# Weight halves by q and k, ten layer-norm applies on GpSimd, and a last tile in two PSUM banks: one change to a one-core attention-plus-gMLP kernel

## The chip, the cores and the metric

The kernel runs on one core of one Trainium2 chip. The metric is the device time of one execution in microseconds (us). The profile and the trace are of one profiled execution; they cover the span from the first to the last instruction, which is mostly about 1.7 us shorter than the device time. Five engines matter: TensorE (PE, with its weight loads PEld), VectorE (DVE), ScalarE (ACT), GpSimd (POOL) and SyncE (SP), which issues most DMAs (transfers; one "lands" when its data is in place). PSUM is the memory into which TensorE writes its results.

Here a run counts as slow when it is more than 1.5% above the fastest run of the same kernel.

## The reference, cut to what matters

```python
x = A_x                                   # [1, 2048, 512] bf16
xn = _layernorm(x, axis=-1, eps=1e-05)
return x + _A_ref(xn, A_wqkv, A_wo) + _B_ref(xn, B_w_in, B_w_sp, B_b_sp, B_w_out)
# _A_ref: qkv = xn @ wqkv; 32 heads of 16; each position attends to 8 positions, 2 apart; softmax; @ wo
# _B_ref: z = gelu(xn @ w_in); z2 = layernorm(second half); (z1 * (w_sp @ z2 + b)) @ w_out
```

## The kernel before

The 16 tiles of 128 tokens are taken in four blocks of four tiles (block j holds tiles j, j+4, j+8, j+12). A tile passes through batch-norm statistics, square root, reciprocal and the *apply* (subtract the mean, multiply by the reciprocal), then a transpose to `xnT`. Six tiles are transposed by TensorE and copied out of PSUM by ScalarE, the other ten by DMA transposes from SP. TensorE then multiplies `xnT` with the q/k weights (tile `pq`), later with the z2 weights (`pz`). VectorE multiplies q with shifted k (the *products*, into `r_pr`), and TensorE sums those into logits (`pl`).

```python
def load_wqk(E, h):                       # half h: q and k columns of chunks 2h, 2h+1
    ...
    for s in range(2):
        E.dma_start(w[:, :, s, 2 * h:2 * h + 2, :], src[:, :, s, 2 * h:2 * h + 2, :])

load_wqk(SP, 0)
SP.dma_start(xall[:, 1], xblk[1])
load_wqk(SP, 1)
for j in range(2, 4):
    SP.dma_start(xall[:, j], xblk[j])
SP.dma_start(w_z2[:], ...)
# ... [cut]
def ln_apply(i):
    j, tb = i % 4, i // 4
    V.tensor_scalar(xall[:, j, tb, :], xall[:, j, tb, :], mv[:, i, 0:1], rstd[:, i:i + 1],
                    ALU.subtract, ALU.mult)
def tr_dma(i):
    SP.dma_start_transpose(xnT[:, :, i * P:(i + 1) * P], xall[:, j, tb, :])
# ... [cut: first block]
qk_part(pqs[1], 0, 1, 0, 2)
tr_copy(t0[3], tr(t0[3]))
qk_part(pqs[2], 0, 2, 0, 2)               # stands between the 4th tile's transposes and their readers
# ... [cut]
ln_stats_blk(2)
ln_recip(blk_cols(2))
for i in blk(2):
    ln_apply(i)
    tr_dma(i)
# ... [cut: q/k of block 1, block 3 in the same way]
for c in range(C):                        # the products start
    prod_c(0, c)
    prod_c(1, c)
z2s(0, 0)
z2s(0, 1)
for c in range(C):
    qk_mm(2, c)                           # needs all four tiles of block 2
logits(0)
logits(1)
# ...
qk_mm(3, 0)                               # needs all four tiles of block 3
# ... [cut: the last tile's output]
store(3, A, slice(0, D // 2))             # two adds after the last matmul
store(3, SP, slice(D // 2, D))
```

Of the kernel before, what the change touches and what calls it, by code (L numbers as in the profile page):

```python
# [8 lines left out]
F32 = mybir.dt.float32  # L9
I32 = mybir.dt.int32  # L10
ACT = mybir.ActivationFunctionType
ALU = mybir.AluOpType
# [3 lines left out]
P = 128  # L16
S = 2048
D = 512
NT = S // P
TB = 4  # L20
TBS = 512
C = D // P
# [4 lines left out]
HALO = 16  # L27
F = 1376
FH = 688
FHALF = 344  # L30
MCH = 7
FPAD = MCH * P
FULL = (MCH - 2) * P
KR = (FH - FULL) // 2
# [7 lines left out]
APPLY_PER_G = [1, 2, 3, 4, 4, 4, 4, 4, 4, 6, 6, 6, 4, 4, 3, 1]  # L42
OUT_AFTER = [8, 12, 15.5]
NZ1 = 8


def slot_w(s):
# [4 lines left out]
def kernel(  # L52
# [13 lines left out]
    V = nc.vector  # L66
    A = nc.scalar
    G = nc.gpsimd
    PE = nc.tensor
    SP = nc.sync  # L70
# [7 lines left out]
    ps_mm = ctx.enter_context(tc.tile_pool(name="ps_mm", bufs=3, space=PSUM))  # L78
# [5 lines left out]
    xall = r_x[:, 0:4 * TB * D].rearrange("p (j b d) -> p j b d", j=4, b=TB)  # L84
    vp = r_x[:].rearrange("p (d t) -> p d t", d=DH)
    r_w = sb.tile([P, 8192], BF16, name="r_w")
    wqk = r_w[:, 0:4096].rearrange("p (k f) -> p k f", k=C)
    wv = r_w[:, 4096:6144].rearrange("p (k h d) -> p k d h", k=C, d=DH)
    a_sb = r_w[:, 0:4096].rearrange("p (w t) -> p w t", w=W)
    wout = r_w[:, 4096:4096 + MCH * D].rearrange("p (m n) -> p m n", m=MCH)  # L90
    r_qk = sb.tile([P, 2 * C * (HALO + S)], BF16, name="r_qk")
    qk = r_qk[:].rearrange("p (c s t) -> p c s t", s=2, c=C)
    wsp = [r_qk[:, n * 2048:(n + 1) * 2048].rearrange("p (k t) -> p k t", k=NT) for n in range(NWSP)]
    xr_t = [r_qk[:, NWSP * 2048 + n * D:NWSP * 2048 + (n + 1) * D] for n in range(4)]
    ot_t = [r_qk[:, NWSP * 2048 + (4 + n) * D:NWSP * 2048 + (5 + n) * D] for n in range(4)]
    r_lg = sb.tile([P, W * TBS], F32, name="r_lg")
    lg = r_lg[:].rearrange("p (w o t) -> p w o t", w=W, o=4)
    wo_r = r_lg[:].bitcast(BF16).rearrange("p (d n) -> p d n", d=DH)
# [3 lines left out]
    op = r_pr[:, 8192:16384].rearrange("p (d t) -> p d t", d=DH)  # L102

    xnT = sb.tile([P, C, S], BF16, name="xnT")
    w_z2 = sb.tile([P, C, FH], BF16, name="w_z2")
    w_z1 = sb.tile([P, C, FH], BF16, name="w_z1")
    z2 = sb.tile([P, NT, FH], BF16, name="z2")
    z1u = sb.tile([P, NZ1, FPAD], BF16, name="z1u")
    smt = sb.tile([P, 4, 256], F32, name="smt")
    uT = sb.tile([P, 2, MCH, TBS], BF16, name="uT")  # L110
# [8 lines left out]
    mv = sb.tile([P, NT, 2], F32, name="mv")  # L119
    rstd = sb.tile([P, NT], F32, name="rstd")  # L120
# [9 lines left out]
    def load_x0(E, tb, p0=0, p1=P):  # L130
        E.dma_start(xall[p0:p1, 0, tb, :], x2[tb * TBS + p0:tb * TBS + p1, :])  # L131

    def load_wqk(E, h):

        w = wqk.rearrange("p k (s c f) -> p k s c f", s=2, c=C)
        src = A_wqkv[:, 0:2 * D].rearrange("(k p) (s c f) -> p k s c f", p=P, s=2, c=C)
        for s in range(2):
            E.dma_start(w[:, :, s, 2 * h:2 * h + 2, :], src[:, :, s, 2 * h:2 * h + 2, :])  # L138

    load_x0(SP, 0, 0, 64)  # L140
    load_x0(A, 0, 64, P)
# [6 lines left out]
    load_wqk(SP, 1)  # L148
    for j in range(2, 4):
        SP.dma_start(xall[:, j], xblk[j])  # L150
    SP.dma_start(w_z2[:], B_w_in[:, FH:F].rearrange("(k p) f -> p k f", p=P))


    V.memset(warm[:], 0.0)
# [26 lines left out]
    def ln_recip(sl):  # L181
        V.reciprocal(rstd[:, sl], rstd[:, sl])

    def ln_apply(i):
        j, tb = i % 4, i // 4
        V.tensor_scalar(xall[:, j, tb, :], xall[:, j, tb, :], mv[:, i, 0:1], rstd[:, i:i + 1],
                        ALU.subtract, ALU.mult)

    def tr(i):
        j, tb = i % 4, i // 4  # L190
        pt = ps_aux.tile([P, C, P], BF16, name="pt", tag="aux")
        for c in range(C):
            PE.transpose(pt[:, c, :], xall[:, j, tb, c * P:(c + 1) * P], ident[:])  # L193
        return pt

    def tr_copy(i, pt):
        A.copy(xnT[:, :, i * P:(i + 1) * P], pt[:])  # L197
# [54 lines left out]
    def z1_mm(n):  # L252
        i = 4 * (n % 4) + ORD[n // 4]
        pz = zmm(i, w_z1)
        z = 32 * (n % 4)
        A.activation(z1u[:, n % NZ1, z:z + FH].rearrange("p (a b) -> p a b", a=2), pz[:, :, 0:FHALF],  # L256
                     ACT.Gelu_apprx_tanh)

    def qk_part(pq, j, c, b0, b1):

        xv = xnT[:].rearrange("p k (b j t) -> p k b j t", b=TB, j=4)
        for s in range(2):
            for kc in range(C):
                PE.matmul(pq[:, s, b0 * P:b1 * P], wqk[:, kc, s * D + c * P:s * D + (c + 1) * P],  # L264
                          xv[:, kc, b0:b1, j, :], start=(kc == 0), stop=(kc == C - 1))

    def qk_copy(pq, j, c):
        dst = qk[:, c, :, HALO:HALO + S].rearrange("p s (b j t) -> p s b j t", b=TB, j=4)
        A.copy(dst[:, :, :, j, :], pq[:].rearrange("p s (b t) -> p s b t", b=TB))  # L269

    def qk_tile():
        return ps_mm.tile([P, 2, TBS], F32, name="pq", tag="mm")

    def qk_mm(j, c):
        pq = qk_tile()
        qk_part(pq, j, c, 0, TB)
        qk_copy(pq, j, c)
# [105 lines left out]
    def u_mul(n, gs):  # L383
        s = n % NZ1
        g = gs[:].rearrange("p a b -> p (a b)")

        z = 32 * (n % 4)
        V.tensor_tensor(z1u[:, s, 0:FULL], g[:, 0:FULL], z1u[:, s, z:z + FULL], ALU.mult)
        rest = z1u[:, s, FULL:FPAD].rearrange("p (a q) -> p a q", a=2)[:, :, z:z + KR]
        V.tensor_tensor(rest, g[:, FULL:FH].rearrange("p (a q) -> p a q", a=2),  # L390
                        z1u[:, s, z + FULL:z + FH].rearrange("p (a q) -> p a q", a=2), ALU.mult)
        SP.dma_start_transpose(uT[:, (n // 4) % 2, :, (n % 4) * P:(n % 4 + 1) * P], z1u[:, s, :])
# [6 lines left out]
    def out_mm(o, last=False):  # L399
        pos = []  # L400
        for tb in range(TB):
            if last and tb >= 2:
                pa = ps_aux.tile([P, TBS], F32, name="pa", tag="aux")
                pos.append(pa[:])
                continue
            if tb % 2 == 0:
                pmm = ps_mm.tile([P, 2, TBS], F32, name="po", tag="mm")
            pos.append(pmm[:, tb % 2, :])
        for d in range(DH):
            for tb in range(TB):  # L410
                PE.matmul(pos[tb], op[32 * tb:32 * tb + 32, d, o * P:(o + 1) * P],  # L411
                          wo_r[32 * tb:32 * tb + 32, d, :],
                          start=(d == 0), stop=False, tile_position=(32 * tb, 0))
        for rt in range(2):
            for tb in range(TB):
                q, m = 32 * tb, MCH - 2 + rt
                PE.matmul(pos[tb], uT[q:q + KR, o % 2, m, tb * P:(tb + 1) * P], wout[q:q + KR, m, :],  # L417
                          start=False, stop=False, tile_position=(q, 0))

        def store(tb, E, cs):  # L420
            i = 4 * tb + ORD[o]
            V.tensor_tensor(ot_t[tb][:, cs], pos[tb][:, cs], xr_t[tb][:, cs], ALU.add)  # L422
            E.dma_start(out2[i * P:(i + 1) * P, cs], ot_t[tb][:, cs])

        for h in range(2):
            pair = (2 * h, 2 * h + 1)
            alone = last and h == 1
            for tb in pair:
                for m in range(MCH - 2):
                    PE.matmul(pos[tb], uT[:, o % 2, m, tb * P:(tb + 1) * P], wout[:, m, :],  # L430
                              start=False, stop=(m == MCH - 3))
                if alone and tb == 2:
                    store(2, SP, slice(0, D))
            if alone:
                store(3, A, slice(0, D // 2))
                store(3, SP, slice(D // 2, D))
            else:
                for tb in pair:
                    store(tb, SP, slice(0, D))


    pwm = ps_aux.tile([P, TBS], F32, name="pwm", tag="aux")
# [1 line left out]
    def blk(j):  # L444
        return [4 * tb + j for tb in range(TB)]

    def col(i):
        return slice(i, i + 1)
# [18 lines left out]
    def warm_up(n):  # L467
        for _ in range(n):
            PE.matmul(pwm[:], warm[:, 0:P], warm[:], start=True, stop=True)

    def ln_tile(i):
        ln_recip(col(i))
        ln_apply(i)

    t0, i1 = blk(0), blk(1)
    warm_up(9)
    for n in range(2):
# [2 lines left out]
    for n in range(2):  # L480
        ln_tile(t0[n])
        tr_copy(t0[n], tr(t0[n]))
        if n == 0:
            warm_up(2)
    for n in range(2, 4):
        ln_stats(t0[n])
        ln_sqrt(col(t0[n]))
    for n in range(2, 4):
        ln_tile(t0[n])
    pqs = [qk_tile() for _ in range(3)]  # L490
    qk_part(pqs[0], 0, 0, 0, 2)
    tr_copy(t0[2], tr(t0[2]))
    qk_part(pqs[1], 0, 1, 0, 2)
    tr_copy(t0[3], tr(t0[3]))
    qk_part(pqs[2], 0, 2, 0, 2)
    for n in range(2):
        ln_stats(i1[n])
    ln_sqrt(slice(1, 8, 4))
# [1 line left out]
    ln_recip(slice(1, 8, 4))  # L500
    ln_apply(i1[0])
    ln_apply(i1[1])
    ln_stats(i1[3])
    qk_part(pqs[0], 0, 0, 2, 4)
    qk_copy(pqs[0], 0, 0)
    ln_sqrt(slice(9, 16, 4))
    ln_recip(slice(9, 16, 4))
    for n in range(2, 4):
        ln_apply(i1[n])
        tr_dma(i1[n])  # L510
    qk_part(pqs[1], 0, 1, 2, 4)
    qk_copy(pqs[1], 0, 1)
    for n in range(2):
        tr_copy(i1[n], tr(i1[n]))
    qk_part(pqs[2], 0, 2, 2, 4)
    qk_copy(pqs[2], 0, 2)
    qk_mm(0, 3)
    ln_stats_blk(2)
    ln_recip(blk_cols(2))
    for i in blk(2):  # L520
        ln_apply(i)
        tr_dma(i)
    pqs = [qk_tile() for _ in range(3)]
    for c in range(3):
# [6 lines left out]
            ln_recip(blk_cols(3))  # L531
    qk_mm(1, 3)
    for i in blk(3):
        ln_apply(i)
        tr_dma(i)
    SP.dma_start(r_w[:, 4096:6144].rearrange("p (k f) -> p k f", k=C),
                 A_wqkv[:, 2 * D:3 * D].rearrange("(k p) f -> p k f", p=P))
# [80 lines left out]
    for n in range(NT):  # L618
        o = n // 4
# [43 lines left out]
```

## Time and profile before

| | before |
|---|---|
| device time, median of the first 3 runs | 210.86 us (210.77 to 211.06) |
| profiled span | 209.3 us |
| PE busy | 202.7 us, 97% |
| DVE busy | 176.9 us, 85% |
| POOL busy | 5.7 us, 3% |

The page of the kernel before: the span, the engines' busy times, and the busy tenths in 40 slices of 5.2 us. PEclk is the granted TensorE clock in tenths.

```profile
span 209.3 us, 4186 instructions
...
PE 202.7 (97%) x1727; PEld 121.3 (58%) x1731; DVE 176.9 (85%) x267; ACT 92.9 (44%) x148; POOL 5.7 (3%) x21
...
PE   7799999999999999999999999999999999999993
...
POOL 7000001100000000000000000000000000000000
PEclk9999999999999999999999999999999999999999
```

TensorE is full from the third slice to the last but one, at full clock. The chain of waits of the kernel before says the same in order of time (start, length, what):

```profile
4.61 6.68 DMA r_w<-in_A_wqkv_dram
...
11.34 2.36 PE pq L264 x20
...
14.14 9.57 PE pq L264 x72
23.71 2.41 PE pz L207 x16
```

From 11.34 us on, every step of the chain is TensorE work, down to 206 us, but for gaps of at most 0.16 us.

The timeline of the kernel before (start, length, engine, line, operation, tiles, shapes, count; in brackets the idle time before and what ended it). These are lines, each from the list of its engine:

```profile
13.98 9.73 PE L264 MATMUL pq<-xnT,r_w 128*128 128x256 bf16 x72
23.54 2.57 PE L207 MATMUL pz<-w_z,xnT 128*128 128x344 bf16 x16
...
34.96 1.90 PE L264 MATMUL pq<-xnT,r_w 128*128 128x512 bf16 x8
...
24.09 1.38 DVE L186 TENSOR_SCALAR r_x<-r_x,mv,rstd 128x512 bf16<-128x512 bf16 x4
25.39 3.49 DVE L287 TENSOR_TENSOR r_pr<-r_qk 128x2048 bf16<-128x2048 bf16 x3
...
14.84 14.88 SPq L201 DMA_TRANSPOSE xnT<-r_x  x10
```

The last block's four applies take VectorE 1.38 us together (0.41 us for one by itself), then the products start (the list is cut at 28 us; the first products run on after it). All ten DMA transposes are issued by 29.7 us; the last q/k matmuls that need them start at 34.96.

The tail on VectorE before, the last line of its list (two adds):

```profile
206.01 0.76 DVE L422 TENSOR_TENSOR r_qk<-pa,r_qk 128x256 bf16<-128x256 f32 x2 [0.27 <-PE pa L430]
```

### The profile page before, as it was taken

How to read it: one execution, taken by the hardware profiler on the slowest of the kernel's cores; microseconds unless marked ns; L12 is line 12 of the kernel's file. 1: busy time of each engine (PE TensorE's matmuls, PEld its weight loads, DVE VectorE, ACT ScalarE, POOL GpSimd, SP SyncE). 2: the span in 40 equal slices, each digit the busy share in tenths (PEclk: the TensorE clock that was granted, in tenths of full speed). 3: DMA queues.
4: the chain of work that ended last, by engine and by line, in shares of the span. 5: the costliest groups of instructions: out<-in, count | busy, mean ns of one | idle time of the engine just before them, and what ended most of it. 6: DMA issues, size and time to landing. Idle time of an engine off the chain costs nothing.

```text
span 209.3 us, 4186 instructions
## 1 busy us (share of the span) xinstructions
PE 202.7 (97%) x1727; PEld 121.3 (58%) x1731; DVE 176.9 (85%) x267; ACT 92.9 (44%) x148; POOL 5.7 (3%) x21
## 2 busy tenths in 40 slices
PE   7799999999999999999999999999999999999993
PEld 2578644545566566666666666456666446664441
DVE  3888997969999987999999999859999979991404
ACT  3475797788997897941431223102123102231000
POOL 7000001100000000000000000000000000000000
PEclk9999999999999999999999999999999999999999
DMA  4984556000000499799999776994833234424153
GB/s 132 326 281 66 101 94 232 0 0 3 0 3 0 103 179 210 146 280 216 177 191 218 129 161 145 147 194 150 126 76 89 47 94 150 47 45 89 51 152 100
DMA packets 66914, 25.91 MB, mean 124 GB/s; under 512 B 56080, under 2 KB 66768, under 8 KB 66768
## 3 DMA queue, kind: packets, MB, share of 16 engines
q1 hardware_dynamic: 66304, 25.20, 56.1%
q10 hardware_dynamic: 592, 0.46, 0.7%
q8 instruction: 13, 0.21, 0.4%
q14 instruction: 5, 0.04, 0.1%
HBM read 10.13 MB, written 2.10 MB: 58 GB/s over the span
## 4 chain that ended last, share of the span: by engine, by line
PE 93%; DMA 3%; SPq 2%; issue 1%; DVE 0%; DVEq 0%
PE pg L377 36%; PE pz L207 18%; PE pq L264 12%; PE po L430 7%; PE po L411 7%; PE pv L342 7%; PE pl L304 4%; DMA r_w<-in_A_wqkv_dram 3%; PE pa L430 1%; PE po L417 1%; SPq L138 1%; SPq L131 1%; SPq L147 0%; PE pt L193 0%; DVE r_qk L422 0%
## 5 line engine op out<-in xcount | busy, mean ns | idle before, releaser
L377 PE MATMUL pg<-z,r_qk 128*128 128x344 bf16 x512 | 76.8, 309 | 0.0
L377 PEld LDWEIGHTS <-r_qk 128*128 128x128 bf16 x512 | 50.0, 98 | 24.9 <-issue 0.4
L207 PE MATMUL pz<-w_z,xnT 128*128 128x344 bf16 x256 | 40.9, 309 | 0.0
L380 ACT ACTIVATE gs<-pg,b_col 128x688 bf16<-128x688 f32 x16 | 13.3, 832 | 57.0 <-PE pg L377 50.1
L353 DVE TENSOR_TENSOR r_pr<-r_x,r_w 128x2048 bf16<-128x2048 bf16 x32 | 38.1, 1221 | 0.3
L357 DVE TENSOR_TENSOR r_pr<-r_pr 128x2048 bf16<-128x2048 bf16 x28 | 33.8, 1219 | 0.1
L207 PEld LDWEIGHTS <-xnT 128*128 128x128 bf16 x256 | 24.6, 98 | 14.7 <-issue 2.0
L264 PE MATMUL pq<-xnT,r_w 128*128 128x256 bf16 (+1 forms) x176 | 29.4, 321 | 0.8 <-ACT xnT L197 0.7
L297 DVE TENSOR_TENSOR r_pr<-r_qk 128x2048 bf16<-128x2048 bf16 x24 | 27.5, 1218 | 2.8 <-ACT r_qk L269 2.8
L264 PEld LDWEIGHTS <-r_w 128*128 128x128 bf16 x176 | 16.8, 98 | 11.5 <-issue 1.8
L422 DVE TENSOR_TENSOR r_qk<-po,r_qk 128x512 bf16<-128x512 f32 x14 | 9.0, 686 | 15.6 <-PE po L430 15.6
L256 ACT ACTIVATE z1u<-pz 128x688 bf16<-128x688 f32 x16 | 11.9, 742 | 20.8 <-PE pz L207 20.7
L269 ACT CAST r_qk<-pq 128x1024 bf16<-128x1024 f32 x16 | 15.8, 1012 | 5.8 <-PE pq L264 4.3
L430 PE MATMUL po<-r_w,uT 128*128 128x512 bf16 x66 | 14.9, 379 | 0.6 <-issue 0.6
L342 PE MATMUL pv<-xnT,r_w 128*32 128x512 bf16 x256 | 14.7, 380 | 0.0
L411 PE MATMUL po<-r_lg,r_pr 32*128 32x512 bf16 x224 | 14.5, 375 | 0.0
L430 PEld LDWEIGHTS <-uT 128*128 128x128 bf16 x80 | 7.5, 98 | 10.2 <-issue 1.7
L175 DVE BATCH_NORM_STATS2 stats<-r_x 128x6 f32<-128x512 bf16 x16 | 10.8, 672 | 2.3 <-DMA r_x<-in_A_x_dram 2.1
L219 ACT ACTIVATE junk<-z 128x688 bf16<-128x688 bf16 x16 | 12.4, 778 | 0.5
L213 ACT ACTIVATE z<-pz 128x688 bf16<-128x688 f32 x16 | 11.8, 736 | 1.9 <-PE pz L207 1.9
L342 PEld LDWEIGHTS <-r_w 128*32 128x32 bf16 x256 | 9.5, 139 | 4.5 <-issue 0.3
L411 PEld LDWEIGHTS <-r_pr 32*128 32x128 bf16 x256 | 6.2, 93 | 7.7 <-issue 1.3
(67 smaller groups left out, 136.3 us busy)
## 6 DMA issues: line engine op xcount, KB each, us to landing
r_lg<-in_A_wo_dram SPq DMA_DIRECT2D x4, 512.0 KB, 9.0
r_qk<-in_A_x_dram SPq DMA_DIRECT2D x16, 128.0 KB, 2.2
out_dram<-r_qk SPq DMA_DIRECT2D x15, 128.0 KB, 1.7
r_x<-in_A_x_dram SPq DMA_DIRECT2D x3, 512.0 KB, 6.0
w_z<-in_B_w_in_dram SPq DMA_DIRECT2D x2, 688.0 KB, 5.3
r_w<-in_A_wqkv_dram SPq DMA_DIRECT2D x4, 256.0 KB, 6.4
r_w<-in_B_w_out_dram SPq DMA_DIRECT2D x1, 640.0 KB, 5.6
r_w<-in_A_wqkv_dram SPq DMA_DIRECT2D x1, 512.0 KB, 4.0
```

Of the source, the lines that this page charges most:

```text
L207: PE.matmul(pz[:, hh, 0:FHALF], xnT[:, kc, i * P:(i + 1) * P], wz[:, kc, hh * FHALF:(hh + 1) * FHALF], start=(kc == 0), stop=(kc == C - 1))
L219: A.activation(junk[:], z2[:, i, :], ACT.Square, accum_out=zsq[:, q:q + 1])
L264: PE.matmul(pq[:, s, b0 * P:b1 * P], wqk[:, kc, s * D + c * P:s * D + (c + 1) * P], xv[:, kc, b0:b1, j, :], start=(kc == 0), stop=(kc == C ...
L269: A.copy(dst[:, :, :, j, :], pq[:].rearrange("p s (b t) -> p s b t", b=TB))
L297: V.tensor_tensor(pr[g % 2][:, :, ww], q4, k4, ALU.mult)
L342: PE.matmul(pv[32 * tb:32 * tb + 32, dd, :], wv[:, kc, 2 * d2 + dd, :], xnT[:, kc, tb * TBS:(tb + 1) * TBS], start=(kc == 0), stop=(kc == ...
L353: V.tensor_tensor(pw_t[n], vp[:, :, off:off + P], a_sb[:, slot_w(w), ts].unsqueeze(1).broadcast_to([P, DH, P]), ALU.mult)
L357: V.tensor_tensor(pw_t[n] if dst is None else dst, pw_t[n], pw_t[m], ALU.add)
L377: PE.matmul(pg[:, hh, 0:FHALF], wsp[n % NWSP][:, k, :], z2[:, k, hh * FHALF:(hh + 1) * FHALF], start=(q == 0), stop=(q == NT - 1))
L380: A.activation(gs[:], pg[:, :, 0:FHALF], ACT.Identity, bias=b_col[:, i:i + 1])
L411: PE.matmul(pos[tb], op[32 * tb:32 * tb + 32, d, o * P:(o + 1) * P], wo_r[32 * tb:32 * tb + 32, d, :], start=(d == 0), stop=False, tile_po ...
L430: PE.matmul(pos[tb], uT[:, o % 2, m, tb * P:(tb + 1) * P], wout[:, m, :], start=False, stop=(m == MCH - 3))
```

## The change

Its intent: load the q/k weights as two column halves, q and then k (rows of 1 KB instead of 512 B, two loads fewer), and let TensorE begin with q alone; take ten applies off VectorE, which is 85% busy, and give them to GpSimd, which is idle; issue the z2 weights after the second block's transposes; and split the last tile's output over two PSUM banks, so that most of its add runs before the last matmul. Cut to its core:

```diff
-    def load_wqk(E, h):
-        ...
-        for s in range(2):
-            E.dma_start(w[:, :, s, 2 * h:2 * h + 2, :], src[:, :, s, 2 * h:2 * h + 2, :])
+    def load_wqk(E, s):
+        E.dma_start(wqk[:, :, s * D:(s + 1) * D], A_wqkv[:, s * D:(s + 1) * D]...)
     ...
-    SP.dma_start(w_z2[:], ...)                      # moved, see below
     ...
-    def ln_apply(i):
+    def ln_apply(i, E=V):
-        V.tensor_scalar(...)
+        E.tensor_scalar(...)
     ...
+    LN_E = G
     ...
-        if n == 0:
-            warm_up(2)
     ...
+    halves = [(0, 0), (0, 2), (1, 0)]               # q chunks 0,1; q 2,3; k 0,1
-    qk_part(pqs[0], 0, 0, 0, 2)
+    qk2_part(pqs[0], *halves[0], 0, 2)
+    qk2_part(pqs[1], *halves[1], 0, 2)
     tr_copy(t0[2], tr(t0[2]))
-    qk_part(pqs[1], 0, 1, 0, 2)
+    qk2_part(pqs[2], *halves[2], 0, 2)
     tr_copy(t0[3], tr(t0[3]))
-    qk_part(pqs[2], 0, 2, 0, 2)
     ...
     for n in range(2, 4):
-        ln_apply(i1[n])
+        ln_apply(i1[n], LN_E)                       # the same for blk(2) and blk(3): ten tiles
         tr_dma(i1[n])
+    SP.dma_start(w_z2[:], ...)
     ...
+        if last:
+            cuts[3] = [(pos[3][:, 0:LASTCUT], slice(0, LASTCUT)), (pb[:, 0, 0:D - LASTCUT], slice(LASTCUT, D))]
```

More of the change, by code (lines that the diff above doesn't have):

```diff
@@ L44 @@
 NZ1 = 8
+LASTCUT = 288
 def slot_w(s):
@@ L131, in load_x0 @@
         E.dma_start(xall[p0:p1, 0, tb, :], x2[tb * TBS + p0:tb * TBS + p1, :])
-    def load_wqk(E, h):
-        w = wqk.rearrange("p k (s c f) -> p k s c f", s=2, c=C)
-        src = A_wqkv[:, 0:2 * D].rearrange("(k p) (s c f) -> p k s c f", p=P, s=2, c=C)
-        for s in range(2):
-            E.dma_start(w[:, :, s, 2 * h:2 * h + 2, :], src[:, :, s, 2 * h:2 * h + 2, :])
+    def load_wqk(E, s):
+        E.dma_start(wqk[:, :, s * D:(s + 1) * D],
+                    A_wqkv[:, s * D:(s + 1) * D].rearrange("(k p) f -> p k f", p=P))
     load_x0(SP, 0, 0, 64)
@@ L150 @@
         SP.dma_start(xall[:, j], xblk[j])
-    SP.dma_start(w_z2[:], B_w_in[:, FH:F].rearrange("(k p) f -> p k f", p=P))
     V.memset(warm[:], 0.0)
@@ L182, in ln_recip @@
         V.reciprocal(rstd[:, sl], rstd[:, sl])
-    def ln_apply(i):
+    def ln_apply(i, E=V):
         j, tb = i % 4, i // 4
-        V.tensor_scalar(xall[:, j, tb, :], xall[:, j, tb, :], mv[:, i, 0:1], rstd[:, i:i + 1],
+        E.tensor_scalar(xall[:, j, tb, :], xall[:, j, tb, :], mv[:, i, 0:1], rstd[:, i:i + 1],
                         ALU.subtract, ALU.mult)
@@ L265, in qk_part, with qk2_part, qk2_copy @@
                           xv[:, kc, b0:b1, j, :], start=(kc == 0), stop=(kc == C - 1))
+    def qk2_part(pq, s, c0, b0, b1):
+        xv = xnT[:].rearrange("p k (b j t) -> p k b j t", b=TB, j=4)
+        for cc in range(2):
+            for kc in range(C):
+                PE.matmul(pq[:, cc, b0 * P:b1 * P],
+                          wqk[:, kc, s * D + (c0 + cc) * P:s * D + (c0 + cc + 1) * P],
+                          xv[:, kc, b0:b1, 0, :], start=(kc == 0), stop=(kc == C - 1))
+    def qk2_copy(pq, s, c0):
+        dst = qk[:, c0:c0 + 2, s, HALO:HALO + S].rearrange("p c (b j t) -> p c b j t", b=TB, j=4)
+        A.copy(dst[:, :, :, 0, :], pq[:].rearrange("p c (b t) -> p c b t", b=TB))
     def qk_copy(pq, j, c):
@@ L404, in out_mm @@
                 pos.append(pa[:])
+                if tb == 3:
+                    pb = ps_mm.tile([P, 2, TBS], F32, name="pb", tag="mm")
                 continue
@@ L408, in out_mm @@
             pos.append(pmm[:, tb % 2, :])
+        cuts = [[(pos[tb], slice(0, D))] for tb in range(TB)]
+        if last:
+            cuts[3] = [(pos[3][:, 0:LASTCUT], slice(0, LASTCUT)), (pb[:, 0, 0:D - LASTCUT], slice(LASTCUT, D))]
         for d in range(DH):
             for tb in range(TB):
-                PE.matmul(pos[tb], op[32 * tb:32 * tb + 32, d, o * P:(o + 1) * P],
-                          wo_r[32 * tb:32 * tb + 32, d, :],
-                          start=(d == 0), stop=False, tile_position=(32 * tb, 0))
+                for pc, cs in cuts[tb]:
+                    PE.matmul(pc, op[32 * tb:32 * tb + 32, d, o * P:(o + 1) * P],
+                              wo_r[32 * tb:32 * tb + 32, d, cs],
+                              start=(d == 0), stop=False, tile_position=(32 * tb, 0))
         for rt in range(2):
@@ L416, in out_mm, with store, finish @@
                 q, m = 32 * tb, MCH - 2 + rt
-                PE.matmul(pos[tb], uT[q:q + KR, o % 2, m, tb * P:(tb + 1) * P], wout[q:q + KR, m, :],
-                          start=False, stop=False, tile_position=(q, 0))
-        def store(tb, E, cs):
+                for pc, cs in cuts[tb]:
+                    PE.matmul(pc, uT[q:q + KR, o % 2, m, tb * P:(tb + 1) * P], wout[q:q + KR, m, cs],
+                              start=False, stop=False, tile_position=(q, 0))
+        def store(tb, E, part):
             i = 4 * tb + ORD[o]
-            V.tensor_tensor(ot_t[tb][:, cs], pos[tb][:, cs], xr_t[tb][:, cs], ALU.add)
+            pc, cs = part
+            V.tensor_tensor(ot_t[tb][:, cs], pc, xr_t[tb][:, cs], ALU.add)
             E.dma_start(out2[i * P:(i + 1) * P, cs], ot_t[tb][:, cs])
+        def finish(tb, part):
+            pc, cs = part
+            for m in range(MCH - 2):
+                PE.matmul(pc, uT[:, o % 2, m, tb * P:(tb + 1) * P], wout[:, m, cs],
+                          start=False, stop=(m == MCH - 3))
         for h in range(2):
             pair = (2 * h, 2 * h + 1)
-            alone = last and h == 1
-            for tb in pair:
-                for m in range(MCH - 2):
-                    PE.matmul(pos[tb], uT[:, o % 2, m, tb * P:(tb + 1) * P], wout[:, m, :],
-                              start=False, stop=(m == MCH - 3))
-                if alone and tb == 2:
-                    store(2, SP, slice(0, D))
-            if alone:
-                store(3, A, slice(0, D // 2))
-                store(3, SP, slice(D // 2, D))
+            if last and h == 1:
+                for tb, part, E in ((2, cuts[2][0], SP), (3, cuts[3][0], A), (3, cuts[3][1], SP)):
+                    finish(tb, part)
+                    store(tb, E, part)
             else:
                 for tb in pair:
-                    store(tb, SP, slice(0, D))
+                    finish(tb, cuts[tb][0])
+                for tb in pair:
+                    store(tb, SP, cuts[tb][0])
     pwm = ps_aux.tile([P, TBS], F32, name="pwm", tag="aux")
@@ L503 @@
     ln_stats(i1[3])
-    qk_part(pqs[0], 0, 0, 2, 4)
-    qk_copy(pqs[0], 0, 0)
+    for n in range(2):
+        qk2_part(pqs[n], *halves[n], 2, 4)
+        qk2_copy(pqs[n], *halves[n])
     ln_sqrt(slice(9, 16, 4))
@@ L508 @@
     for n in range(2, 4):
-        ln_apply(i1[n])
+        ln_apply(i1[n], LN_E)
         tr_dma(i1[n])
-    qk_part(pqs[1], 0, 1, 2, 4)
-    qk_copy(pqs[1], 0, 1)
+    SP.dma_start(w_z2[:], B_w_in[:, FH:F].rearrange("(k p) f -> p k f", p=P))
     for n in range(2):
         tr_copy(i1[n], tr(i1[n]))
-    qk_part(pqs[2], 0, 2, 2, 4)
-    qk_copy(pqs[2], 0, 2)
-    qk_mm(0, 3)
+    qk2_part(pqs[2], *halves[2], 2, 4)
+    qk2_copy(pqs[2], *halves[2])
+    pq3 = qk_tile()
+    qk2_part(pq3, 1, 2, 0, 4)
+    qk2_copy(pq3, 1, 2)
     ln_stats_blk(2)
@@ L520 @@
     for i in blk(2):
-        ln_apply(i)
+        ln_apply(i, LN_E)
         tr_dma(i)
@@ L533 @@
     for i in blk(3):
-        ln_apply(i)
+        ln_apply(i, LN_E)
         tr_dma(i)
```

## The prediction

> **What bounds it now.** TensorE. The page gives PE 97% of 209.3 us, DVE 85%, ACT 44%, POOL 3%. The chain of waits is PE work from 11.34 to 206.0 us; before that it runs through the q/k weight load (landing 11.29). Real matmuls start (timeline) at 8.46 and idle once, 11.1 to 11.34, for that load. So only the start, the tail after 206.0, and new PE waits count.
>
> **Start.**
> - Two warm-up matmuls go. They run 6.29 to 7.14 and hold back the second tile's transposes (start 7.41; input ready at 6.35). The first q matmul can start at about 7.75 instead of 8.46: -0.7.
> - q/k weights: before, each quarter pair with 512 B rows took 1.76 us to land; x blocks with 1 KB rows take 1.5 us per 512 KB. I estimate q at 7.3 and k at 10.4 (before: last quarter 11.29). But the new order needs all of k after 16 matmuls (16 x 0.109 us, so about 9.7): PE waits about 0.7 there.
> - The fourth tile's transposes now come directly before the matmuls that read them. Transpose to copied data takes 1.06 us (10.43 to 11.49): about 0.8 of new idle. Net by then: about +0.5.
> - Tiles 2 and 3 of the second block: their square root stands behind two PSUM copies of 1.0 us, their apply is on GpSimd (estimate 0.75 us, from POOL's affine selects, 0.29 us at 128 and 0.21 at 32 columns; 0.41 on DVE), and two DMA transposes (1.2 us issue each, 2.5 to landing) follow. Landing about 20.4, wanted at 19.75: +0.7.
> - Clock: the Trainium skill, "TensorE: Matmul & The Clock Gate", Part 1, says the array runs at half rate until a busy window of about 3.4 us. The trace agrees: 512-column matmuls start 0.427 us apart up to 6.72 us, 256-column ones 0.109 apart from 8.46. Without the warm-ups the first 16 q matmuls may run at 0.213: up to +0.7 more, one in two.
>
> **Middle.** DVE loses ten applies (3.5 us) and starts the products about 2 us earlier; PE doesn't. The skill's "GPSIMD Engine Reference", section 1, names contention with DVE instructions of two SBUF inputs. The trace agrees: a POOL cast of 16 columns took 1.05 us beside a product, ending with it. So the last block's four applies should take 1 to 2 us each beside products, and still land before PE wants them (about 35 us). The z2 weights, issued about 19, landing about 23.7 (other such loads take 4.0 and 5.3), just make it.
>
> **Tail.** Before: last matmul, two adds of 0.42, 0.33 apart, then the store. After: one 224-column add after PE: -0.35. Against that, 18 more row-tiled and 5 more full matmuls: about +0.2. Net -0.1.
>
> **Sum.** Start +1.2 (+0.7 in half the cases), tail -0.1, and -0.4 for waits overestimated: 211.9 us, range 210.3 to 213.6. Faster by over 2%: 0.02; within: 0.91; slower: 0.07.
>
> **Signs.** Right: new PE idle for k weights near 10, for the ACT copy near 11.5, for a DMA transpose near 20; z2 matmuls after 24.0 (before 23.54); POOL applies 0.75 us beside batch-norm statistics, longer beside products; one add after the last matmul. Wrong: z2 matmuls before 23.5, or q matmuls 0.109 apart from the first.
>
> **What would make it wrong.** k landing before 9.8; faster GpSimd applies; GpSimd starved by products, so that the last block comes late and PE stalls; split matmuls costing more.

## The result, and the profile after

The changed kernel took 223.81 us median of 4 runs (220.24 to 227.12) against 210.81 us (210.48 to 211.06) in the same rounds. The ratio is the mean time of one kernel's fast runs over the mean of the other's fast runs in the same rounds, so it is not quite the ratio of the medians: 1.052, 95% interval 1.045 to 1.059. It is slower by 5%, and the predicted range (210.3 to 213.6 us) missed it.

The page of the changed kernel, the lines that answer to those of before, and its group of applies (busy time, mean ns of one, idle before):

```profile
span 225.4 us, 4233 instructions
...
PE 207.2 (92%) x1752; PEld 124.6 (55%) x1752; DVE 174.2 (77%) x257; ACT 93.1 (41%) x148; POOL 34.5 (15%) x31
...
PE   7686999149999999999999999999999999999994
...
POOL 7019999910000000000000000000000000000000
PEclk9999699956999999999999999999999999999999
...
L183 POOL TENSOR_SCALAR r_x<-r_x,mv,rstd 128x512 bf16<-128x512 bf16 x10 | 29.6, 2971 | 10.7 <-DVE rstd L179 10.7
```

One apply on GpSimd takes 2971 ns on average, not 410. POOL is full for five slices; the ten applies run from 16 to 46 us. TensorE has a hole at the eighth slice, and PEclk drops in two places, each after an idle stretch.

The chain of waits of the changed kernel, where it now runs through GpSimd:

```profile
16.22 3.70 POOL r_x L183 x2
...
20.34 25.46 POOL r_x L183 x8
...
45.81 2.41 DMA xnT<-r_x
...
48.36 3.57 PE pq L261 x8
```

The timeline of the changed kernel on TensorE, the same steps as before:

```profile
17.51 2.78 PE L261 MATMUL pq<-xnT,r_w 128*128 128x256 bf16 x24
22.85 6.19 PE L261 MATMUL pq<-xnT,r_w 128*128 128x256 bf16 x32 [2.55 <-DMA xnT<-r_x]
28.87 2.50 PE L204 MATMUL pz<-w_z,xnT 128*128 128x344 bf16 x16
...
48.36 3.57 PE L261 MATMUL pq<-xnT,r_w 128*128 128x512 bf16 x8 [8.24 <-DMA xnT<-r_x]
```

Setting the starts beside those of before tells where the 16.1 us of this profiled run went:

| step | before | after | lag | new since the last row |
|---|---|---|---|---|
| the 72 q/k matmuls after the second block's TensorE transposes | 13.98 | 14.91 | 0.9 | waits for k weights and for a PSUM copy |
| first z2 matmul | 23.54 | 28.87 | 5.3 | 2.6 idle for two transposes, 1.7 low clock |
| first logits | 33.12 | 38.20 | 5.1 | |
| last block's first q/k matmul | 34.96 | 48.36 | 13.4 | 8.2 idle for the last transposes |
| first spatial matmul (`pg`) | 83.45 | 99.70 | 16.3 | 2.9 low clock after the idle time |
| end of the span | 209.3 | 225.4 | 16.1 | tail shorter by 0.13 |

The low clock can be counted from the matmul starts: after the wait of 2.6 us, some fifteen matmuls of 256 columns start 0.213 us apart instead of 0.109; after the wait of 8.2 us, the 512-column ones start 0.427 us apart instead of 0.216.

The applies are not all alike. Two single lines of the changed kernel's timeline, GpSimd, and the VectorE list for the same time:

```profile
16.22 2.07 POOL L183 TENSOR_SCALAR r_x<-r_x,mv,rstd 128x512 bf16<-128x512 bf16 x1 [10.74 <-DVE rstd L179]
...
28.55 5.06 POOL L183 TENSOR_SCALAR r_x<-r_x,mv,rstd 128x512 bf16<-128x512 bf16 x1
...
27.23 9.56 DVE L296 TENSOR_TENSOR r_pr<-r_qk 128x2048 bf16<-128x2048 bf16 x8
```

The first six applies, 16.2 to 28.6 us, took 2.07 us each: they began while VectorE ran batch-norm statistics or nothing. (The sixth was under way when the products began at 27.23, and was not slowed.) Their starts are 2.06 us apart, so the length does not hang on where the profiler marks an end. Those that began while VectorE ran products took 5.06, 4.97 and 5.18 us; in other traces below, such applies took 4.2 to 5.1. The ninth began in the pause between two groups of products and took 2.07.

The tail of the changed kernel on VectorE, the last line of its list:

```profile
222.32 0.39 DVE L440 TENSOR_TENSOR r_qk<-pb,r_qk 128x224 bf16<-128x224 f32 x1
```

One add of 0.39 us follows the last matmul, instead of two.

This profiled run was a slow one (227.12 us), and so was the one profiled when the kernel ran again. So nothing below rests on its length alone: the same waits are in the traces of fast runs of three experiments, `before_pool`, `first_six` and `last_four`.

### The profile page after: what moved, and what is told of

The parts are those of the page before. It is cut to its first block, busy times and chain, and to the rows that moved or that the text cites. A ratio compares the mean times of both kernels' runs of the same rounds, so it can differ in the third digit from the quotient of the medians.

```text
span 225.4 us, 4233 instructions
## 1 busy us (share of the span) xinstructions
PE 207.2 (92%) x1752; PEld 124.6 (55%) x1752; DVE 174.2 (77%) x257; ACT 93.1 (41%) x148; POOL 34.5 (15%) x31
## 3 DMA queue, kind: packets, MB, share of 16 engines
q1 hardware_dynamic: 65248, 25.19, 50.5%
## 4 chain that ended last, share of the span: by engine, by line
PE 76%; POOL 13%; DMA 4%; issue 4%; SPq 1%; DVE 1%; DVEq 0%; POOLq 0%
PE pg L386 33%; PE pz L204 16%; POOL r_x L183 13%; PE po L446 7%; PE pv L351 6%; PE po L427 6%; PE pq L261 4%; DMA r_x<-in_A_x_dram 3%; PE pl L313 3%; DMA xnT<-r_x 1%; DVE r_qk L440 1%; PE po L434 1%; PE pb L427 1%; SPq L132 1%; SPq L135 0%
## 5 line engine op out<-in xcount | busy, mean ns | idle before, releaser
L204 PE MATMUL pz<-w_z,xnT 128*128 128x344 bf16 x256 | 42.0, 315 | 0.0
L261 PE MATMUL pq<-xnT,r_w 128*128 128x512 bf16 (+1 forms) x120 | 25.2, 374 | 10.8 <-DMA xnT<-r_x 10.8
L183 POOL TENSOR_SCALAR r_x<-r_x,mv,rstd 128x512 bf16<-128x512 bf16 x10 | 29.6, 2971 | 10.7 <-DVE rstd L179 10.7
L261 PEld LDWEIGHTS <-r_w 128*128 128x128 bf16 x120 | 12.7, 108 | 22.3 <-issue 11.0
L278 ACT CAST r_qk<-pq 128x1024 bf16<-128x1024 f32 x12 | 12.0, 1010 | 19.5 <-PE pq L261 19.4
L446 PE MATMUL po<-r_w,uT 128*128 128x512 bf16 x70 | 15.8, 380 | 0.0
L446 PEld LDWEIGHTS <-uT 128*128 128x128 bf16 x85 | 8.0, 98 | 9.8 <-issue 1.5
```

The costliest lines, as they stand in the source:

```text
L183: E.tensor_scalar(xall[:, j, tb, :], xall[:, j, tb, :], mv[:, i, 0:1], rstd[:, i:i + 1], ALU.subtract, ALU.mult)
L204: PE.matmul(pz[:, hh, 0:FHALF], xnT[:, kc, i * P:(i + 1) * P], wz[:, kc, hh * FHALF:(hh + 1) * FHALF], start=(kc == 0), stop=(kc == C - 1))
L261: PE.matmul(pq[:, s, b0 * P:b1 * P], wqk[:, kc, s * D + c * P:s * D + (c + 1) * P], xv[:, kc, b0:b1, j, :], start=(kc == 0), stop=(kc == C ...
L446: PE.matmul(pc, uT[:, o % 2, m, tb * P:(tb + 1) * P], wout[:, m, cs], start=False, stop=(m == MCH - 3))
```

## The experiments

Theory A: the applies are long on GpSimd (2.07 us, and 5 us beside products), so the DMA transposes behind them come late and TensorE waits. Theory B, the rival, which the prediction had leaned on: the new order of loads and matmuls at the start costs the time. Twelve kernels ran, all correct against the reference. The medians are of all runs, slow ones too; the ratios are of fast runs alone.

| run | edit | median us | ratio to before (95%) |
|---|---|---|---|
| after_again | the changed kernel | 223.62 | 1.053 (1.047 to 1.060) |
| after_dve | changed, ten applies back on VectorE | 212.35 | 1.009 (1.006 to 1.012) |
| before_pool | before, ten applies on GpSimd | 220.24 | 1.045 (1.037 to 1.052) |
| pool_forms | before, scratch GpSimd work | 213.40 (1 run) | none |
| first_six | changed, only the first six on GpSimd | 217.31 | 1.029 (1.023 to 1.035) |
| last_four | changed, only the last four on GpSimd | 222.10 | 1.054 (1.048 to 1.061) |
| after_filled | changed, both long waits filled with matmuls | 226.49 | 1.073 (1.067 to 1.079) |
| filled_last | changed, only the last wait filled | 223.66 | 1.060 (1.058 to 1.062) |
| tail_only | before, the tail split | 210.40 | 0.998 (0.994 to 1.002) |
| dve_early_z2 | after_dve, z2 weights issued early | 212.46 | 1.008 (1.007 to 1.010) |
| dve_warm | after_dve, warm-up matmuls kept | 212.55 | 1.010 (1.007 to 1.014) |
| mended | after_dve, four edits against the new waits at the start | 210.92 | 1.001 (0.998 to 1.003) |

### The changed kernel again

No edit. Expected:

> The changed kernel once more, unaltered, for its spread and for a profile in its fast state. Theory A (the ten applies on GpSimd are long: 2.07 us beside batch-norm statistics, 5 us beside products, so the transposes come late and TensorE waits, then runs at a low clock): 219 to 227 us again, six applies of 2.07 us, a wait of several us before the first q/k matmuls of the last block. Theory B (the new order of loads and q/k matmuls, and the late z2 weights, cost the time): the same total, but with the waits before 24 us making up most of it.

Measured: 220.74 to 225.33 us, median 223.62; before 210.43. The six applies beside statistics took 2.07 us again. The loss repeats, and so does the spread; the hoped-for profile of a fast run did not come, the profiled one was of 225.33 us.

### All applies back on VectorE

```diff
-    LN_E = G
+    LN_E = V
```

> The changed kernel with all ten applies back on VectorE. Theory A: nearly all of the loss goes; what stays is the start (first q/k matmuls of the second block 17.5 instead of 16.6, +0.9) less the tail (-0.2): 211 to 212 us. Theory B: the loss stays, 217 us or more.

Measured: 212.35 us. By fast runs alone (means), the changed kernel trailed by 11.3 us in these rounds (221.81 against 210.52), and 9.3 of them go with this one line (212.47). The timeline of this run (a fast one) on TensorE, where the changed kernel had its two long waits:

```profile
21.08 4.52 PE L261 MATMUL pq<-xnT,r_w 128*128 128x256 bf16 x32 [0.16 <-DMA xnT<-r_x]
...
37.35 1.90 PE L261 MATMUL pq<-xnT,r_w 128*128 128x512 bf16 x8
```

The wait of 2.55 us is down to 0.16, and the one of 8.24 is gone. Theory B keeps 1.9 us (212.35 less 210.43), more than the 0.6 to 1.6 expected; the last runs below look into that.

### The kernel before with the ten applies on GpSimd

```diff
-        V.tensor_scalar(xall[:, j, tb, :], ...)
+        E.tensor_scalar(xall[:, j, tb, :], ...)
     ...
-        ln_apply(i)
+        ln_apply(i, G)        # ten tiles
```

> The kernel before with the ten applies on GpSimd as the only edit. Theory A: slower by nearly the whole loss, 217 to 225 us, with the wait for the last block's transposes. Theory B: within 1 us of the kernel before.

Measured: 220.24 us, ratio 1.045. The move to GpSimd by itself, without any other part of the change, costs about 9.7 of the 11.3 us (means of fast runs). The timeline of this run (a fast one) on TensorE, and its sixth apply on GpSimd:

```profile
20.99 4.52 PE L264 MATMUL pq<-xnT,r_w 128*128 128x256 bf16 x32 [1.62 <-DMA xnT<-r_x]
...
32.22 9.26 PE L264 MATMUL pq<-xnT,r_w 128*128 128x512 bf16 x32 [4.38 <-DMA xnT<-r_x]
...
24.66 4.92 POOL L186 TENSOR_SCALAR r_x<-r_x,mv,rstd 128x512 bf16<-128x512 bf16 x1
```

The longest wait sits elsewhere than in the changed kernel. The start is quicker here, so the products begin earlier, and already the sixth apply, the last of the third block, meets them. The wait falls on the third block's q/k matmuls (32.22). Which block pays depends on which apply meets the products.

### GpSimd work that nothing waits for

```diff
+    fin, fout, fsc = ...                      # scratch tiles, set once
+    form(512); form(512); form(256); form(128)           # the apply, two pointer scalars
+    form(512, two=False); form(512, ptr=False); form(512, two=False, ptr=False)
+    G.tensor_copy(fout[:], fin[:])
     ...
+    for _ in range(4): form(512)              # while VectorE runs products
```

> The kernel before with extra GpSimd work on scratch tiles that nothing waits for: beside batch-norm statistics, applies of 512, 512, 256 and 128 columns with two pointer scalars, then 512 columns with one operation, with constants in place of pointers, and a copy; beside products, four applies of 512. Theory A: 2.07 us for 512 columns, proportional to columns (about 1.05 at 256, 0.55 at 128, so 4 ns a column), 4 to 5 us each beside products, products stretched by about 0.4 us once per apply, and the kernel's time within 1 us of before. If instead a fixed cost makes the 2.07 us, 128 columns take over 1.5 us. Which form is cheaper is open; a copy should be the cheapest.

The timeline of this run on GpSimd: five single lines from the early part (512, 256 and 128 columns; one operation; a copy), then one beside products:

```profile
6.08 2.07 POOL L180 TENSOR_SCALAR fout<-fin,fsc 128x512 bf16<-128x512 bf16 x1
...
10.42 1.22 POOL L180 TENSOR_SCALAR fout<-fin,fsc 128x256 bf16<-128x256 bf16 x1
11.74 0.79 POOL L180 TENSOR_SCALAR fout<-fin,fsc 128x128 bf16<-128x128 bf16 x1
12.63 1.57 POOL L182 TENSOR_SCALAR fout<-fin,fsc 128x512 bf16<-128x512 bf16 x1
...
18.02 0.61 POOL L191 COPY fout<-fin 128x512 bf16<-128x512 bf16 x1
...
39.57 4.90 POOL L180 TENSOR_SCALAR fout<-fin,fsc 128x512 bf16<-128x512 bf16 x1
```

From 128 to 512 columns an apply grows from 0.79 to 2.07 us: 3.3 ns a column, and 0.37 us that does not depend on the columns. One operation instead of two takes 1.57, constants instead of pointers 1.93 (one operation with a constant 1.65), a plain copy 0.61. So the affine selects of the start-up code, from which the prediction had drawn its 0.75 us, are no measure for an apply: at 128 columns a select took 0.29 us and an apply 0.79. All four applies beside products took 4.7 to 4.9 us, though nothing waited for them and they waited for nothing: the 5 us are a cost of being beside products. In the trace one product takes 1.63 us instead of 1.22 during three of these four applies, so VectorE pays 0.4 us each time.

Two expectations failed. The time is not proportional to the columns (0.55 us was expected at 128), and the kernel took 213.40 us and not within 1 us of before. The extra work reached VectorE's applies at the start. One line of the VectorE list (0.41 us in the kernel before):

```profile
5.10 1.02 DVE L207 TENSOR_SCALAR r_x<-r_x,mv,rstd 128x512 bf16<-128x512 bf16 x1
```

An apply on VectorE beside GpSimd work can be slowed too, this one to 1.02 us, the next to 0.76. But of the eight VectorE applies beside the scratch work only four were slowed (0.60 to 1.02 us); the others took 0.40 to 0.41. In the trace the first q matmul started 0.5 us late (8.96 instead of 8.46), and the first 17 q/k matmuls then ran 0.213 us apart instead of 0.109, about 1.8 us more; by the second block's q/k matmuls the lag was 2.4 us (16.36 instead of 13.98), the same as that of the span. It was one run, so its total is given no weight.

### Only the first six, only the last four

```diff
     for i in blk(3):
-        ln_apply(i, LN_E)
+        ln_apply(i, V)        # first_six; last_four: LN_E = V, and G here
```

> The changed kernel with the last block's four applies back on VectorE and the first six left on GpSimd. Theory A (late transposes), by size: the first six run beside batch-norm statistics at 2.07 us, except the last one or two, and hold VectorE's last four back little; the second block's transposes still land about 2.7 us late and the clock drops there (1.7 us), but the wait of 8 us for the last block goes, with its 2.9 us of low clock: 214.5 to 217.5 us.

> The changed kernel with the first six applies back on VectorE and the last four left on GpSimd. GpSimd is free when they come, at about 26 us, but all four then run beside products, 5 us each: the last lands near 46 us. Contention as the cause of the long wait: 219 us or more, three or four applies of 5 us. If it is only the queue of ten that makes the last block late: four applies of 2.07, ending near 34, and 212 to 214 us.

Measured: first_six 217.31 us. All six applies took 2.07 us, none met a product. This is the price of the plain length, 5.0 us over the all-VectorE version (217.31 less 212.35, from other rounds on another chip; the kernel before took 210.74 and 210.43 in the two, but spread from 210.32 to 213.60 in the rounds of first_six), in the upper part of what was expected. last_four 222.10 us, 9.8 us over it. GpSimd is free when these four come, so no queue of ten explains it. The timeline of last_four (a fast run), two of its applies and the wait:

```profile
25.29 5.06 POOL L183 TENSOR_SCALAR r_x<-r_x,mv,rstd 128x512 bf16<-128x512 bf16 x1 [19.79 <-DVE rstd L179]
30.33 4.96 POOL L183 TENSOR_SCALAR r_x<-r_x,mv,rstd 128x512 bf16<-128x512 bf16 x1
...
44.12 3.53 PE L261 MATMUL pq<-xnT,r_w 128*128 128x512 bf16 x8 [7.97 <-DMA xnT<-r_x]
```

The four take 16.3 us instead of VectorE's 1.4 for the same four, and TensorE waits 8 us. (Not all four met products, as had been expected: the third began in a pause and took 2.07 us, the fourth 4.21.) By fast runs the parts do not add up: 5.0 and 9.8 us apart, 9.3 together. So the last four alone cost as much as all ten. Why is not shown, as no fast run of the changed kernel was profiled; its two traces, of slow runs, have the wait for the last block at full length (8.24 and 7.15 us) beside the wait of 2.55 us in the middle.

### Filling the waits with matmuls

```diff
+    fill(11)                  # before the second block's later half; only in after_filled
     ...
     prods(3)
+    fill(28)                  # both kernels
     qk_mm(3, 0)
```

> The changed kernel with matmuls on constant data, results unused, put into its two long TensorE waits: 11 before the second block's later half (2.4 us at full clock) and 28 before the last block (6.0 us). No wait gets shorter by it. If the clock that drops after idle costs what the record shows (q/k matmuls of 256 columns 0.213 us apart instead of 0.109, of 512 columns 0.427 instead of 0.216), 3 to 5 us come back: 217 to 221 us beside about 223 of the changed kernel, and its matmuls keep 0.109 and 0.216 throughout. If the clock is no cost of its own: no change.

Measured: 226.49 us, the slowest of all. A miss, and a telling one. The first filling did what it should: the second block's matmuls ran at full clock and the z2 matmuls started at 27.25 instead of 28.87. But the products then began earlier and met the sixth apply, which took 4.92 us instead of 2.07. The third block's matmuls waited 4.3 us until 34.01. (The profile puts this wait to a ScalarE step; but the sixth apply ended at 31.5, and a transpose takes 2.4 us or more to land.) The clock fell there instead, and the last block's q/k matmuls started at 50.28, later than in the changed kernel. The timeline of this run on TensorE at that place (`pf` is the filling):

```profile
44.23 6.22 PE L494 MATMUL pf<-warm 128*128 128x512 bf16 x27
50.28 1.89 PE L261 MATMUL pq<-xnT,r_w 128*128 128x512 bf16 x8
```

No idle time stands before 50.28: it is the second filling itself that holds the last block back. The last block's transposes landed at 46.05 us by the profile, 2.2 us earlier than in the changed kernel (48.22), but the wait had moved to the third block, and the 28 matmuls no longer filled one. About 4.2 us (50.28 less 46.05) are thus the experiment's own. Without them it would have come to about 222 us, by this estimate, no better and no worse than the changed kernel. So this run does not say what the low clock costs. The next expectation gives the collision with the sixth apply as the whole reason, which the trace does not bear out.

> The changed kernel with matmuls on constant data only in the last of its long TensorE waits (28, about 6 us at full clock, before the first q/k matmuls of the last block). The run with both fillings got slower, 226.5 us, and its record shows why: the second block's matmuls ran at full clock, so the products began earlier and met the sixth GpSimd apply (4.9 us). This one leaves everything up to the products as in the changed kernel. Theory A: the last block's first matmuls run at 0.216 us apart instead of 0.427 and 2 to 3 us come back, 219 to 221.5 us. If the low clock costs nothing: about 223.

Measured: 223.66 us, no less than the changed kernel. Also a miss in the total. The timeline of this run (a fast one) on TensorE:

```profile
47.62 1.89 PE L261 MATMUL pq<-xnT,r_w 128*128 128x512 bf16 x8 [1.05 <-DMA xnT<-r_x]
```

Here the filling ended before the transposes landed, so it held nothing back. The 8 matmuls of the last block start 0.216 us apart here, and from the first of them to the first spatial matmul it is 48.5 us (47.62 to 96.09), against 51.3 and 50.5 us in the two traces of the changed kernel. So the low clock costs 2 to 3 us at that place. The total does not show it: the traced run's span of 221.8 us is shorter than the two traced ones of the changed kernel (225.4 and 222.8), but those were slow runs, and the fast runs of the changed kernel (220.2 to 223.1 us) are no longer than the fast ones here (223.3 to 223.8). What the low clock is worth in the total stays open.

### The tail alone

```diff
+            cuts[3] = [(pos[3][:, 0:LASTCUT], slice(0, LASTCUT)), (pb[:, 0, 0:D - LASTCUT], slice(LASTCUT, D))]
```

> The kernel before with the last tile's output in two PSUM banks as the only edit. Both theories: from the last weight matmuls on 0.1 to 0.2 us shorter (one add after the last matmul instead of two, less the extra matmuls): 210.2 to 210.4 us, ratio 0.999.

Measured: 210.40 against 210.74 us, ratio 0.998 with an interval that includes 1. In the traces the stretch from the first spatial matmul to the end is 125.84 us before, 125.70 in the changed kernel and 125.53 here. It is a gain of 0.1 to 0.3 us that the total can't confirm.

### The start: what is left with VectorE applies

```diff
     SP.dma_start(xall[:, j], xblk[j])
+    SP.dma_start(w_z2[:], ...)               # here again
     ...
-    SP.dma_start(w_z2[:], ...)               # on top of LN_E = V
```

> The changed kernel with all applies on VectorE and the z2 weights issued at the start as in the kernel before. In the record of the all-VectorE run the z2 matmuls waited 0.5 us for these weights (landing 25.1). Expected 0.3 to 0.6 us less than that run: 211.7 to 212.1 us. Under theory B, that the late z2 weights are a large part of the loss: 1 us or more less.

Measured: 212.46 us against 212.35 for after_dve, no gain. The wait in front of the second group of z2 matmuls is still there with the weights long landed. Its timeline, on TensorE and on ScalarE:

```profile
26.13 1.33 PE L205 MATMUL pz<-w_z,xnT 128*128 128x344 bf16 x8 [0.41 <-ACT r_qk L279]
...
24.88 0.30 ACT L177 ACTIVATE rstd<-mv,eps_t 128x4 f32<-128x4 f32 x1 [1.83 <-DVE mv L174]
25.09 1.91 ACT L279 CAST r_qk<-pq 128x1024 bf16<-128x1024 f32 x2
```

The z2 matmul waits for a PSUM buffer that the q/k copy on ScalarE has to empty. That copy stands behind the last block's square root, which waits for VectorE's statistics, and those are late because the whole start is. The reading "the late z2 weights cost 0.5 us" was wrong.

```diff
     tr_copy(t0[n], tr(t0[n]))
+        if n == 0:                           # on top of LN_E = V
+            warm_up(2)
```

> The changed kernel with all applies on VectorE and the two warm-up matmuls of the kernel before kept. In the all-VectorE run the first q/k matmuls ran at the low clock (first k part 0.19 us apart, 0.65 us lost), in the run of the changed kernel they did not. Expected: first q matmul at about 8.3 instead of 7.7, which the wait for the k weights at 10.7 hides, no low clock after it, 0.2 to 0.6 us less than without: 211.8 to 212.2 us. If the low clock there is chance in either case: no difference.

Measured: 212.55 us, no difference from 212.35. In its trace the first q matmuls run at full clock; the wait for the k weights (to 10.51) and the copy of the fourth tile (to 12.45) remain, and they set the time. In the all-VectorE run without warm-ups the first k matmuls ran 0.19 us apart, in the traces of the changed kernel and of dve_early_z2, also without them, 0.109. So the low clock there comes and goes. It cost about 0.6 us in the trace of after_dve (the next q/k matmuls started at 15.54, against 14.91 in the changed kernel, where the k weights came at the same time), but it does not explain the 1.9 us: the run that kept the warm-ups, and ran there at full clock, was no faster.

### A version with the waits removed

```diff
+    SP.dma_start(w_z2[:], ...)                # at the start again
+            warm_up(2)
+    tr_copy(t0[3], tr(t0[3]))                 # ahead of the first k matmuls
     qk2_part(pqs[2], *halves[2], 0, 2)
-    tr_copy(t0[3], tr(t0[3]))
     ln_stats(i1[3])
+    ln_sqrt(slice(9, 16, 4))                  # ahead of the PSUM copies
```

> A version to beat both: the changed kernel with all applies on VectorE, z2 weights at the start, the two warm-up matmuls kept, the fourth tile's transposes ahead of the first k matmuls (so that its copy is done when they end), and the square root of the second block's later tiles ahead of the PSUM copies. Each wait that the change made at the start is taken away but the one for the k weights. Expected: second block's transposes no longer waited for, z2 matmuls at 23.2 to 23.5, tail 0.13 shorter: 210.0 to 210.6 us, ratio 0.997 to 1.000.

Measured: 210.92 against 210.78 us, ratio 1.001, no difference from the kernel before. It is just outside the expected 210.0 to 210.6, and the z2 matmuls started at 23.96, not at 23.2 to 23.5. The early z2 weights and the warm-ups brought nothing each by itself. With the two changes of order on top of both, the fourth tile's transposes and the square root, the same rounds give about 1.6 us back (212.46 and 212.55 against 210.92). Which of the two brings more was not separated, and the early weights and the warm-ups were not run together without them. No version clearly beat the kernel before.

## Why the prediction was wrong, point by point

**The step that failed.** The prediction put the GpSimd apply at "0.75 us" and said of the last block that its applies "should take 1 to 2 us each beside products, and still land before PE wants them (about 35 us)". Measured: 2.07 us beside statistics, 5 us beside products, and the last transposes landed at 48.2 us. The mechanism, contention with products, was on the list, and a late last block stood under what would make it wrong; the size of an apply was mis-set, alone and beside products. In the sum this is the missing term: 9.3 us between the fast runs of the changed kernel and of its all-VectorE twin, and 9.8 us for the move alone (220.24 less 210.43).

Two errors made it. First, the price of an apply was taken from another operation of the same engine, the affine select. The scratch run shows that operations on GpSimd differ by a factor of 3.4 at the same shape (0.61 for a copy, 2.07 for an apply). Second, the trace of before did show one GpSimd operation beside a product (a 16-column cast, 1.05 us), and the prediction read it as an addition of about one product. For an apply of 512 columns it is 2.9 us (4.97 less 2.07), more than two products. The Trainium skill, "GPSIMD Engine Reference", section 1, names the contention with VectorE instructions of two SBUF inputs; these traces agree, 2.07 against 5 us.

**The clock.** The prediction feared the low clock only for the first q matmuls. In the profiled run of the changed kernel they ran at full clock, which the prediction had listed as a sign against itself. The clock fell later, after waits of 2.6 and 8.2 us. The skill's "TensorE: Matmul & The Clock Gate", under "Why this matters for your kernels", advises against idle gaps over about 3 us; here gaps of 2.5 to 2.6 us were enough in three traces (the changed kernel twice, filled_last), while 1.6 us in before_pool was not.

**What held.** The first q matmul was put at 7.75 us and started at 7.76. The k weights were put at 10.4 and the matmuls that wait for them started at 10.78. The copy that now blocks was put at about 0.8 us of idle, and the profile shows 0.67. The tail was put at -0.1; the trace has -0.13.

**What held for the wrong reason, or not at all.** The transposes of the second block were put at "about 20.4" and TensorE's wait at 0.7; the wait ended at 22.85. With VectorE applies it is 0.3 (21.08 instead of 20.76 in after_dve). The start as a whole was put at +1.2, or +1.9 with a low clock, and the all-VectorE run lies 1.9 us above the kernel before. That is luck: 0.7 of the +1.2 belonged to GpSimd applies, which this run does not have, so its own terms come to +0.5 or +1.2. VectorE was to start the products about 2 us earlier; they began 1.8 us later (27.23 instead of 25.39). The z2 weights were put at landing about 23.7, just in time; they landed at 26.36 in the changed kernel and 25.07 in after_dve, and TensorE got to them later still.

**What stays open.** Why the changed kernel spreads over 7 us: the traces show that a small shift decides which apply meets products, but no fast run of that kernel was profiled, and whether its slow runs are a state of the chip or only this chance is not known. How much of the total the low clock costs. And what of the 5 us of an apply is waiting and what is slower work; the records give only its start and end. Their pattern suggests mostly waiting: of the 20 slowed applies in these traces, 16 ended 0.23 to 0.24 us after a lengthened product (1.62 to 1.71 us) had ended, and the other four ended 1.78 us after the last product before a pause, as if they had then had most of their 2.07 us still to do.

## What to carry to other kernels

Work moved from a busy engine to an idle one is safe only if the results are not sooner needed than the slower engine can give them: here VectorE was no bottleneck, and the ten applies stood directly before the transposes that feed one. Price an operation on its new engine by a run of that very operation there, with the neighbour busy as it will be, and not by another operation of that engine. And before work is put in to fill a wait, ask where the wait will be afterwards: in the version with both fillings the first one moved the later wait to another place, and the second, left without a wait to fill, held TensorE up by about 4 us.

## What the Trainium skill lacked or had wrong

- "GPSIMD Engine Reference", section 4.1 (Engine selection), calls one-input operations "roughly line-rate", and section 3.1 gives 768 ns for 512 elements as a best case. A two-operation apply with per-partition scalars on 128 x 512 bf16 took 2.07 us here (3.3 ns a column and 0.37 us fixed), one operation 1.57 us; only the copy, 0.61 us, is within the 768 ns. VectorE does the same apply in 0.41 us, so the ratio is 5, where that row has about 2 even for two-input operations.
- The same page, section 1, names the contention with VectorE but gives no size; other pages of the skill go further into this contention, but none was found with a size for this pair of operations. Here an apply that starts while VectorE runs 128 x 2048 products took 4.2 to 5.2 us instead of 2.07, and during most of these applies one product took 1.62 to 1.71 us instead of 1.22.
- The same section names VectorE instructions in a 2-port mode as the other contenders, again without a size. In pool_forms four of the eight VectorE applies beside GpSimd work took 0.60 to 1.02 us instead of 0.41, and four did not; whether the apply runs in such a mode no run here shows.
- "TensorE: Matmul & The Clock Gate", "Why this matters for your kernels": no gaps over about 3 us. An idle gap of 2.6 us was followed by 3.2 us at half rate (matmuls of 256 columns 0.213 us apart), beginning 0.7 us after work had resumed; a gap of 1.6 us in before_pool was not.
